# An mLSTM and top-2 expert kernel: the second half of the decay product moves to the states' bank and behind the logits, and five smaller edits

## The chip, the cores and the metric

The kernel runs on one core of a Trainium2 chip. The time is the device time of one execution in microseconds (us); before the change it was 513.11 us, the median of 3 runs (511.17 to 516.01). The core has five engines that take their instructions in order, each from its own queue: TensorE (PE, matrix products; its weight loads are shown as PEld), VectorE (DVE), ScalarE (ACT), GpSimd (POOL) and SyncE (SP, which only starts transfers here; POOL and ACT can start them too). An engine waits for another by semaphores.

## The reference

Two stages follow each other. The first is an mLSTM: for 4 batches and 8 heads a state of 40 x 40 runs through 768 steps, with an exponential input gate and a stabilised forget gate.

```python
for t in range(S):                        # B, H, S, D = 4, 8, 768, 40
    m_new = np.maximum(f_gate[:, :, t] + m, i_gate[:, :, t])
    f_stab = np.exp(f_gate[:, :, t] + m - m_new)
    i_stab = np.exp(i_gate[:, :, t] - m_new)
    C = f_stab * C + i_stab * outer(vt, kt)
    n = f_stab * n + i_stab * kt
    y[:, :, t] = sigmoid(o_gate) * (C @ qt) / max(abs(n . qt), 1)
```

Its 3072 rows of 320 values (8 heads x 40) go into a mixture of experts: `logits = x @ w_gate` plus a noise term that also needs `x @ w_noise`, the two best of 8 experts for each row, and for each expert `relu(x[mask] @ w1[e]) @ w2[e]`, weighted and added up. w1 is 320 x 1024 and w2 1024 x 320 for each expert.

## The kernel before, in words

**Units.** The mLSTM is computed in chunks of L = 64 steps. 768 steps are 12 chunks, and a unit `u` (24 of them) is one chunk of two batches; the two batches are the index `p` of all code below and lie in the two halves of the 128 partitions. Inside a chunk the recurrence is a masked matrix product, between chunks the 40 x 40 states are handed on. The parts of a unit are:

- `e_part(u, ps_)`, L305: the decay product. For each `p` one matmul of 98 rows by 512 columns (L312) of two operands LE and RE gives the exponents of the decays of 64 steps by 8 heads in a bank of the accumulator, and ACT takes the exponential into `w` (L315). Half 0 is `p` = 0, half 1 is `p` = 1. The accumulator's banks are named: `e` for the decay product, `st` for the states, `xt` for transposes and logits, `o` for outputs, `s` for scores (two of two banks). A bank asked for again must first have been read by everybody who uses it.
- `s_part`: the scores, 32 small matmuls and 8 larger ones on PE. `k_part` (L344) and `p_part` (L350, L354): DVE multiplies keys and scores by `w`, into `kd` and `p`.
- `c_part`, L356: 32 small matmuls build the new states in bank `st` (L364), and ACT copies the two batches' states into the next unit's `vk` (L367, two instructions).
- `o_part` (L373): 32 small matmuls give the outputs. `f_part` (L378 to L385): DVE divides, POOL multiplies by the output gate into `xr` (L385). `sig_part` (L320 to L322): three ACT instructions for the output gate.
- `keep_rows` (L388) writes `xr` to DRAM, `t_part` (L396) transposes it on PE, `tc_part` (L400) copies the transposes on ACT, `l_part` (L416) forms the logits on PE.

**Order.** Nothing is scheduled by a planner: each engine does its work in the order in which the Python code emits it. A turn `i` of the loop at the end of the listing works on several units at once: it ends the states and outputs of unit `i`, forms the decays and scores of unit `i + 2` (LEAD is 2), transposes `xr` of unit `i - 1` and forms the logits of unit `i - 2`. Routing (`fill`, `act`, `route`) is put between these parts in small steps: besides, at turn 6 ACT makes five constants, and at six even turns from 8 on it splits a piece of w1 (`split_w1`, L144; POOL makes the low half, L145).

**Gates.** The gates of all steps come by `fi` into `fit` (tile `raw`), in three loads; DVE works them out in pieces of 128 steps (`gate_math`, a scan, sums and a second scan, L193 to L212) into `HL`. Two chunks' worth of them at a time is moved into the operands by `gate_move(k)`, two transfers (L221 into `le`, L222 into `re`); there are two copies of the operands, so move 2 goes where move 0 was and waits until units 0 and 1 have formed their decay products. Moves 0, 1 and 2 serve units 0 and 1, 2 and 3, 4 and 5. The constant rows of RE are made once: `operands` (L228, ACT) and `heads(j, p, engine)` (L235 on ACT, L237 on DVE).

**Rows of the first expert.** Once the ranks of the first 12 units are known, `gather(0, 0, ...)` (L749, POOL) fetches the rows of expert 0 from DRAM by a list of row numbers, one transfer for each 128 rows, three in all, while the last units still run. After the units come the expert layers, a long run of large matmuls.

## Time and profile before

| | |
|---|---|
| median of the runs, us | 513.11 (511.17 to 516.01, n = 3) |
| the profiled execution's own time, us | 511.25 |
| span of its profile, us | 509.5 |
| PE busy | 494.4 us, 97% |
| DVE, ACT, POOL busy | 65%, 49%, 46% |
| PE's decay products | from 11.3 to 121.4 us |
| expert layers | from about 124 us on |

The span is the part of an execution that the profile covers, so 1.75 us of the execution's time lie outside it. PE is busy nearly all the time; the share of the other engines is that over the whole span, and in the units they are busier (the windows below). [...] A timeline row has its start, its length, the engine, the line and the operation, and in brackets the idle time of the engine just before it with the instruction that ended it. "SPq" is the queue of SP.

### The profile page before, as it was taken

To read this page: it belongs to the slowest core of one execution; us is meant where nothing else is said; L and a number is where in the kernel's file an instruction comes from. 1 tells how busy PE (TensorE), PEld (TensorE's weight loads), DVE (VectorE), ACT (ScalarE), POOL (GpSimd) and SP (SyncE) were. 2 spreads that over 40 slices of the span, in tenths; PEclk is the share of its full clock that TensorE was granted. 3 is DMA by queue.
4 is the path that set the end of the run, shared out by engine and by line. 5 is a ranking of instruction groups with operands and counts; after the bars stand their busy time and mean duration, and the time that the engine had idled before them with its cause. 6 is when DMAs were issued, how large, how long until landed. Compare 5 with 4: busy or idle time off the path is not lost.

```text
span 509.5 us, 13368 instructions
## 1 busy us (share of the span) xinstructions
PE 494.4 (97%) x5118; PEld 467.9 (92%) x5118; DVE 331.5 (65%) x891; ACT 248.3 (49%) x598; POOL 233.4 (46%) x313
## 2 busy tenths in 40 slices
PE   8899999999999999999999999999999999999993
PEld 3688888878999998999999999999999999999993
DVE  7998897975987779544853675376448347546310
ACT  6979989978533456414531543254145325415200
POOL 8545686874224863157134605531570453151033
PEclk9989999998999999999999999999999999999998
DMA  6899999988684583495058417723941782461033
GB/s 167 198 250 248 240 252 242 240 218 299 213 261 157 105 177 122 85 278 94 25 108 268 98 28 204 172 68 74 283 87 43 182 187 71 81 158 23 1 41 41
DMA packets 41274, 77.54 MB, mean 152 GB/s; under 512 B 10645, under 2 KB 31068, under 8 KB 39412
## 3 DMA queue, kind: packets, MB, share of 16 engines
q1 hardware_dynamic: 29316, 54.15, 37.5%
q0 software_dynamic: 11616, 20.57, 21.2%
q10 hardware_dynamic: 272, 1.90, 1.1%
q8 instruction: 42, 0.69, 0.6%
q14 instruction: 28, 0.23, 0.1%
HBM read 52.42 MB, written 17.40 MB: 137 GB/s over the span
## 4 chain that ended last, share of the span: by engine, by line
PE 76%; DMA 9%; POOL 4%; issue 3%; DVE 3%; ACT 3%; SPq 1%; POOLq 0%; DVEq 0%; ACTq 0%
PE s L997 25%; DMA y_out<-y,tok 7%; PE e L997 6%; PE o L1025 4%; PE o L1026 4%; PE o L1024 4%; PE o L373 4%; PE st L1025 4%; PE st L1026 4%; PE st L1024 4%; PE e L312 3%; PE s L336 3%; PE st L364 2%; POOL y_out L1052 2%; PE xt L416 2%
## 5 line engine op out<-in xcount | busy, mean ns | idle before, releaser
L1052 POOL DMA_INDIRECT y_out<-y,tok x53 | 87.3, 1647 | 183.1 <-DVE y L1042 180.5
L1009 ACT ACTIVATE hh<-s 128x384 fp32r<-128x384 f32 (+3 forms) x109 | 51.5, 472 | 114.1 <-PE s L997 113.1
L997 PE MATMUL s<-xh,w1h 128*128 128x384 f32 (+6 forms) x327 | 91.8, 336 | 0.0
L1012 DVE SCALAR_TENSOR_TENSOR hlo<-s,hh 128x384 fp32r<-128x384 f32 (+3 forms) x109 | 57.8, 530 | 35.6 <-ACT hh L1009 23.1
L997 PE MATMUL s<-xh,w1l 128*128 128x384 f32 (+6 forms) x327 | 74.1, 335 | 0.0
L749 POOL DMA_INDIRECT xg<-rows,tok x53 | 55.2, 1042 | 27.5 <-issue 14.7
L997 PEld LDWEIGHTS s<-xh,w1h 128*128 128x128 f32 x327 | 58.9, 188 | 1.3
L997 PEld LDWEIGHTS s<-xh,w1l 128*128 128x128 f32 x327 | 57.2, 188 | 1.5 <-DVE xh L783 0.2
L1025 PE MATMUL o<-w2l,hh 128*128 128x320 f32 x184 | 56.8, 309 | 0.0
L1026 PE MATMUL o<-w2h,hlo 128*128 128x320 f32 x184 | 56.8, 308 | 0.0
L1024 PE MATMUL o<-w2h,hh 128*128 128x320 f32 x184 | 56.1, 305 | 0.0
L997 PE MATMUL s<-xl,w1h 128*128 128x384 f32 (+6 forms) x218 | 55.4, 335 | 0.2 <-DVE xl L782 0.2
L1026 PE MATMUL st<-w2h,hlo 128*128 128x320 f32 x168 | 51.9, 309 | 0.0
L1025 PE MATMUL st<-w2l,hh 128*128 128x320 f32 x168 | 51.8, 308 | 0.0
L1024 PE MATMUL st<-w2h,hh 128*128 128x320 f32 x168 | 51.2, 305 | 0.0
L1042 DVE TENSOR_SCALAR y<-o,gw 128x320 f32<-128x320 f32 x22 | 12.1, 551 | 43.4 <-PE o L1026 43.4
L997 PEld LDWEIGHTS s<-xl,w1h 128*128 128x128 f32 x218 | 38.8, 188 | 1.3 <-DVE xl L782 0.4
L385 POOL TENSOR_TENSOR xr<-tm,vk 128x320 f32<-128x320 f32 x24 | 21.1, 880 | 31.6 <-DVE tm L384 7.0
L1042 DVE TENSOR_SCALAR y<-st,gw 128x320 f32<-128x320 f32 x20 | 11.0, 551 | 37.6 <-PE st L1026 37.6
L1024 PEld LDWEIGHTS o<-w2h,hh 128*128 128x128 f32 x184 | 34.5, 188 | 0.0
L1025 PEld LDWEIGHTS o<-w2l,hh 128*128 128x128 f32 x184 | 34.5, 187 | 0.0
L1026 PEld LDWEIGHTS o<-w2h,hlo 128*128 128x128 f32 x184 | 34.5, 187 | 0.0
(248 smaller groups left out, 1177.2 us busy)
## 6 DMA issues: line engine op xcount, KB each, us to landing
vk<-vk_in SPq DMA_DIRECT2D x48, 242.0 KB
raw<-w_in SPq DMA_DIRECT2D x6, 1536.0 KB
raw<-w_in SPq DMA_DIRECT2D x7, 1280.0 KB
qk<-qk_in SPq DMA_DIRECT2D x46, 128.0 KB
y_out<-zrow SPq DMA_DIRECT2D x15, 320.0 KB
rows<-xr POOLq DMA_DIRECT2D x23, 160.0 KB, 4.7
xt__2790<-xb SPq DMA_DIRECT2D x40, 72.0 KB
xt__2790<-xb SPq DMA_DIRECT2D x48, 48.0 KB
```

The source lines that it names most:

```text
L312: T.matmul(ps, LE[j][0:KE, c, 64 - 64 * p:192 - 64 * p], RE[j][0:KE, p, :, c * L:c * L + L], start=True, stop=True)
L373: T.matmul(OQ[u][half[p], h, :], PP[u][n, p, h, :], VK[u % 4][p][n, h * 41:h * 41 + 41], start=True, stop=True)
L385: P.tensor_mul(XR[u], tm.rearrange("p h d -> p (h d)"), SG[u % 4])
L749: P.indirect_dma_start(out=XG[0:rows_of(e, t), t], out_offset=None, in_=XD[0:n], in_offset=bass.IndirectOffsetOnAxis(ap=token(e, t), axis= ...
L997: T.matmul(ps[:, 0:n], l, r, start=i == 0, stop=i == len(ops) - 1)
L1009: A.activation(hi, x, AF.Relu)
L1012: V.scalar_tensor_tensor(lo, x, 0.0, hi.bitcast(F32), op0=OP.max, op1=OP.subtract)
L1024: T.matmul(ps, HH[:, j, c], W2H[:, j], start=j == 0, stop=False)
L1025: T.matmul(ps, HH[:, j, c], W2L[:, j], start=False, stop=False)
L1026: T.matmul(ps, HLO[:, j, c], W2H[:, j], start=False, stop=j == 7)
L1042: V.tensor_scalar(y[0:n], ps[0:n], GW[e][0:n, t:t + 1], None, op0=OP.mult)
L1052: st = P.indirect_dma_start(out=out, out_offset=bass.IndirectOffsetOnAxis(ap=token(e, t), axis=0), in_=y[0:n], in_offset=None, compute_op= ...
```

## The change

1. **Decay product.** From unit 3 on, half 1 of the decay product goes into bank `st`, which it shares with the states, not into `e`, which it shared with half 0. It stands directly behind the logits and the rank products of a turn and ahead of the transposes and the scores; its exponential on ACT stands directly behind that of half 0. In turn 0 (unit 2) it stays behind the scores and in `e`. `sig_part(i + 1)` is now last of the turn's decay and gate work on ACT.
2. **Gathers.** The three gathers are no longer emitted as two and one at the head of a turn, but singly: one at the head of a turn and one behind `f_part`.
3. **Gate rows.** The second load of gates (steps 128 to 383) is the third transfer of the kernel, where it was behind the first unit's keys and queries and a load of constants.
4. **Move 1 and keys of unit 2.** `gate_move(1)` is emitted ahead of `load_unit(2, "k")` on SP's queue.
5. **Move 2** is started by SP, where POOL did.
6. **Head sums.** `heads(1, 0)` is done by ACT, between the exponentials of units 0 and 1, where DVE did it; `heads(1, 1)` now comes behind those of unit 1.

```diff
     SP.dma_start(fit[:, :, 0:128], fi[:, :, 0:128])
     SP.dma_start(cet, ce)
+    SP.dma_start(fit[:, :, 128:384], fi[:, :, 128:384])
...
     load_unit(0, "k")
     SP.dma_start(cs[:, 0:128], cst[:, 0:128])
-    SP.dma_start(fit[:, :, 128:384], fi[:, :, 128:384])
     load_unit(0, "v")
...
-    load_unit(2, "k")
     operands(1, None, A)
     operands(1, 0, A)
     run(gate_math(GC * L, 256))
     gate_move(1)
-    heads(1, 0, V)
+    load_unit(2, "k")
...
         for p in ps_:
-            ps = XTB if first and p else psum.tile([128, 512], F32, name="e")
+            ps = XTB if first and p else psum.tile([128, 512], F32, name="st" if p and u > LEAD else "e")
...
     e_part(0, first=True)
     s_part(1)
+    heads(1, 0, A)
+    e_part(1, first=True)
     heads(1, 1, A)
-    e_part(1, first=True)
     operands(1, 1, A)
...
         if begun and late < len(tiles(0, 0)):
-            gather(0, 0, tiles(0, 0)[late:late + 2])
-            late += 2
-            begun = 2
+            gather(0, 0, tiles(0, 0)[late:late + 1])
+            late += 1
...
         f_part(i, lambda: fill(0.15, False))
+        if begun and late < len(tiles(0, 0)):
+            gather(0, 0, tiles(0, 0)[late:late + 1])
+            late += 1
         if i < 2:
             gate_steps(4)
         if i == 0:
-            gate_move(2, (P, P))
+            gate_move(2)
         t = l_part(i)
         w = r_part(t)
         b = None if w else b_part(t)
         if i:
+            e_part(i + LEAD, (1,))
             t_part(i - 1)
             tc_part(i - 1)
         lc_part(i, t, w)
         bc_part(t, b)
         s_part(i + 2)
         act()
-        if i:
-            sig_part(i + 1)
-        e_part(i + LEAD, (1,))
         if i == 0:
-            sig_part(1)
+            e_part(LEAD, (1,))
+        sig_part(i + 1)
```

On PE, turn 1 of the loop stood so before (states and outputs of unit 1, half 0 of unit 3, transposes of unit 0, scores of unit 3, half 1 of unit 3, states of unit 2):

```order
L364 MATMUL st<-vk_105,kd 40x41 x16
L373 MATMUL o<-vk_105,p 64x41 x16
L312 MATMUL e<-re_93,le_95 128x512
L396 MATMUL xt<-cs,xr 128x128 x3
L333 MATMUL s<-qk_103,cs 64x256 x2
L336 MATMUL s<-qk_103 64x64 x8
L333 MATMUL s<-qk_103,cs 64x256 x2
L336 MATMUL s<-qk_103 64x64 x8
L312 MATMUL e<-re_93,le_95 128x512
L364 MATMUL st<-vk_106,kd 40x41 x16
```

and now so:

```order
L363 MATMUL st<-vk_105,kd 40x41 x16
L372 MATMUL o<-vk_105,p 64x41 x16
L311 MATMUL e<-re_93,le_95 128x512
L311 MATMUL st<-re_93,le_95 128x512
L395 MATMUL xt<-cs,xr 128x128 x3
L332 MATMUL s<-qk_103,cs 64x256 x2
L335 MATMUL s<-qk_103 64x64 x8
L332 MATMUL s<-qk_103,cs 64x256 x2
L335 MATMUL s<-qk_103 64x64 x8
L363 MATMUL st<-vk_106,kd 40x41 x16
```

The second of the two decay products has moved from behind the scores to directly behind the first, and writes bank `st`; later turns have six logit matmuls (L416) between the two. Lines of the changed program are one lower here.

On ACT the first units stood so before (the exponentials of unit 0, head sums, those of unit 1, an operand, the state copies of unit 0, and half 0 of unit 2):

```order
L315 ACTIVATE w<-e 128x512
L315 ACTIVATE w<-xt 128x512
L235 ACTIVATE re_93<-raw_115 32x1024
L315 ACTIVATE w<-e 128x512
L315 ACTIVATE w<-xt 128x512
L228 ACTIVATE re_93<-raw_115 64x1024
L367 ACTIVATE vk_105<-st 40x328 x2
L315 ACTIVATE w<-e 128x512
```

and now so:

```order
L314 ACTIVATE w<-e 128x512
L314 ACTIVATE w<-xt 128x512
L235 ACTIVATE re_93<-raw_115 32x1024
L314 ACTIVATE w<-e 128x512
L314 ACTIVATE w<-xt 128x512
L235 ACTIVATE re_93<-raw_115 32x1024
L228 ACTIVATE re_93<-raw_115 64x1024
L366 ACTIVATE vk_105<-st 40x328 x2
L314 ACTIVATE w<-e 128x512
```

One instruction L235 more stands ahead of the state copies.

On POOL the gathers stood so before, at turns 19 and 20 (rows to DRAM, gathers, output of unit 19; then again for unit 20):

```order
L388 DMA rows<-xr 128x320
L749 DMA xg<-rows,tok 128x336 x2
L385 TENSOR_TENSOR xr<-tm,vk_107 128x320
L388 DMA rows<-xr 128x320
L749 DMA xg<-rows,tok 128x336
L385 TENSOR_TENSOR xr<-tm,vk_104 128x320
```

and now so:

```order
L387 DMA rows<-xr 128x320
L749 DMA xg<-rows,tok 128x336
L384 TENSOR_TENSOR xr<-tm,vk_107 128x320
L749 DMA xg<-rows,tok 128x336
L387 DMA rows<-xr 128x320
L749 DMA xg<-rows,tok 128x336
L384 TENSOR_TENSOR xr<-tm,vk_104 128x320
```

The second gather has moved from ahead of the output of unit 19 to behind it.

## Rows read from the trace of the kernel before

**Rows 1.** Windows (start:end in us, length, busy time of each engine, clock, DMA):

```profile
core 0: us, PE busy (x) PEld busy (x) DVE busy (x) ACT busy (x) POOL busy (x), PEclk, DMA share, GB/s
13.00:15.00 2.00, 0.87 (x13) 0.37 (x7) 1.96 (x4) 1.98 (x3) 1.78 (x5) 1.00 0.58 125
26.45:32.53 6.08, 6.08 (x116) 5.26 (x116) 5.67 (x12) 3.93 (x9) 2.72 (x4) 0.72 0.96 238
40.00:100.00 60.00, 59.37 (x1473) 51.94 (x1472) 52.67 (x149) 53.01 (x135) 42.34 (x72) 1.00 0.97 241
111.71:118.89 7.18, 6.21 (x120) 5.13 (x116) 3.45 (x7) 4.08 (x10) 5.07 (x6) 0.76 0.76 206
124.00:500.00 376.00, 375.49 (x2433) 369.12 (x2432) 227.68 (x633) 145.74 (x360) 149.01 (x174) 1.00 0.51 127
```

**Rows 2.** Chain of waits, 20 to 48 us (start, length, what ran):

```profile
22.57 3.75 DMA re<-hl
...
37.11 0.43 PE e L312
37.54 0.58 PE xt L416 x6
38.12 0.37 PE xt L396 x3
...
41.69 0.43 PE e L312
```

**Rows 3.** Timeline of PE, first units and units 19 to 21:

```profile
14.94 0.81 PE L364 MATMUL st<-vk,kd 64*40 64x41 f32 x32 [1.13 <-DVE kd L344]
...
23.12 0.50 PE L312 MATMUL e<-re,le 98*128 98x512 f32 x1 [0.24 <-ACT w L315]
...
26.45 0.47 PE L312 MATMUL e<-re,le 98*128 98x512 f32 x1 [1.15 <-DMA re<-hl]
...
111.71 0.50 PE L312 MATMUL e<-re,le 98*128 98x512 f32 x1
...
113.76 0.84 PE L396 MATMUL xt<-cs,xr 128*128 128x128 f32 x3 [0.97 <-POOL xr L385]
...
118.89 0.51 PE L312 MATMUL e<-re,le 98*128 98x512 f32 x1
```

**Rows 4.** Timeline of ACT:

```profile
12.96 1.14 ACT L235 ACTIVATE re<-raw 32x1024 fp32r<-32x1024 f32 x1
...
16.32 0.90 ACT L367 ACTIVATE vk<-st 40x328 f32<-40x328 f32 x2
17.85 0.60 ACT L315 ACTIVATE w<-e 128x512 f32<-128x512 f32 x1 [0.64 <-PE e L312]
...
21.68 0.90 ACT L367 ACTIVATE vk<-st 40x328 f32<-40x328 f32 x2
...
40.96 0.89 ACT L367 ACTIVATE vk<-st 40x328 f32<-40x328 f32 x2
...
59.82 0.89 ACT L367 ACTIVATE vk<-st 40x328 f32<-40x328 f32 x2
```

**Rows 5.** Timeline of DVE, gates and first unit:

```profile
7.95 0.48 DVE L193 TENSOR_TENSOR_SCAN xg<-raw,xg 64x128 f32<-64x128 f32 x1 [1.03 <-DMA raw<-fi_in]
...
11.26 0.90 DVE L237 TENSOR_SCALAR re<-raw 32x1024 fp32r<-32x1024 f32 x1
...
14.09 0.79 DVE L344 TENSOR_TENSOR kd<-vk,w 128x640 f32<-128x640 f32 x1
```

**Rows 6.** Timeline of POOL at the gathers:

```profile
111.47 1.31 POOL L749 DMA_INDIRECT xg<-rows,tok  x1 [0.30 <-issue]
112.85 0.86 POOL L385 TENSOR_TENSOR xr<-tm,vk 128x320 f32<-128x320 f32 x1
```

**Rows 7.** Timeline of SP's queue, first units:

```profile
19.54 0.60 SPq L157 DMA_DIRECT2D vk<-vk_in  x1
20.23 2.44 SPq L153 DMA_DIRECT2D qk<-qk_in  x4
```

## The prediction

> **What bounds the kernel now.** I read the windows first. In the expert layers PE is busy 375.49 of 376 us, at full clock and without gaps, and nothing there is changed [rows 1]. The whole of it starts when the last units end, so what the units win or lose is passed on to the end of the program, one for one. In the units, from 40 to 100 us, PE is busy 59.37 of 60 us [rows 1]: the chain of waits runs over PE alone, with 4.58 us from one decay product to the next (37.11 to 41.69) [rows 2]. So the other engines' times don't count there, except where one of them is late. That leaves the places where PE waits. The timeline of PE has three large ones: 1.13 us for `kd` before 14.94, 1.15 us for move 2 before 26.45, and 0.97 us for `xr` before 113.76 [rows 3]. The reader is to see a second cost behind two of them: the granted clock is 0.72 from 26.45 to 32.53 and 0.76 from 111.71 to 118.89, but 1.00 around the wait of 1.13 [rows 1]. [...] The turn from 26.45 to 32.53, from one half 0 to the next, took 6.08 us [rows 1] where an ordinary one takes 4.58 [rows 2]: 1.5 us more, with no wait inside.

> **The change, part by part.** The sum is made against the profiled execution's own time of 511.25, which is 1.86 under the median of 513.11; I carry the difference over to the median.

> *Gathers.* Before, POOL did two gathers ahead of `xr` of unit 19; the second ran from 111.47 to 112.78 and `xr` from 112.85 [rows 6], and PE waited 0.97 for that [rows 3]. The turn from 111.71 to 118.89 took 7.18 us against 4.58 normally, 2.60 lost, of which 0.97 is the wait and the rest the lower clock [rows 1, 3]. Now one gather stands ahead. `xr` can start when the first gather has been issued, 0.30 before the second began at 111.47, thus at about 111.2 (`tm` was long done), and ends at 112.1. PE asks for it behind the logits and the half decay product, which now stands ahead of the transposes: at 113.76 - 0.97 + 0.43 = 113.2. Margin 1.1. What is late next: the second gather now stands behind `xr` and with the rows to DRAM (an issue, 0.6 as in [rows 7]) and the third gather (1.31 by the row of the second) ahead of `xr` of unit 20. From 112.1: 0.3 + 1.3, 0.3 + 0.6, 0.3 + 1.3, then 0.86 of `xr`: it ends at about 117.1 at worst, and PE asks at 113.2 + 4.6 = 117.8. Margin 0.7. Gain **-2.6**; bounds 0 (the stall only moves) and -2.6.

> *First units.* DVE is rid of L237 (0.90) and gets the gate rows earlier, where it waited 1.03 [rows 5]: the load is issued third and no longer eighth. Together 1.9, but `kd` of unit 0 can't start before unit 0's exponentials end, at 12.96 [rows 4]; so it starts 1.1 earlier than 14.09 [rows 5]. PE is free at 14.94 - 1.13 = 13.81 [rows 3], so that wait goes, and outputs of unit 0 and half 0 of unit 2 come 1.1 earlier. That is not kept. ACT has 1.14 more to do (a second L235) ahead of the state copies of unit 0, which began at 16.32 with no idle time before them [rows 4]; now 17.46 to 18.36. The exponential of unit 2 began at 17.85 after 0.64 of idle time [rows 4]; now 18.4, 0.55 later. All of ACT's queue behind it shifts so: the copies of unit 1, 21.68 to 22.58 [rows 4], end at 23.1. Half 1 of unit 3 now needs bank `st`, so it waits for these copies: half 0 of unit 3 ends near 21.5, and PE has a **hole of 1.6 us** until 23.15. From there the old rows give the rest: from the transposes at 38.12 to 41.69 there are 3.57 us [rows 2], with one half product in it as now. Half 0 of unit 4 comes at 26.7, where it came at 26.45: **+0.3**. The hole is longer than the two waits that were followed by the lower clock, so I take that as before (0 change).

> *Move 2 by SP.* It stood on POOL, issued at 22.57 for `re` and landing 3.75 later [rows 2]; PE waited for it. SP is free at 20.14, ahead of unit 4's four loads [rows 7]. Two issues at 0.7 put `re` at about 20.9; landing 3.75 later is 24.7, not late for 26.7, and half as long again would still do. Those loads start at 21.6, not 20.23, and their 2.44 us of issues end at 24.0; the scores of unit 4 need them at about 28.5, so 4.5 us cover them. Cost 0; at worst, if SP's queue makes the move as late as POOL's was, the old wait stays. Move 1 ahead of the loads of unit 2: 4 issues, hidden by the same gap.

> *Half 1 in bank `st`, from unit 4 on.* The instructions are the same, in another order, and PE has 0.63 us idle in 60 [rows 1], so a gain is bounded by 1.0 us over all units. A loss: half 1 must wait until ACT has copied the states. It stands 0.43 + 0.58 = 1.01 behind half 0 [rows 2]; in an ordinary turn the copies end at 40.96 + 0.89 = 41.85 [rows 4], 0.16 behind half 0 at 41.69: margin 0.85. With a piece of w1 between, they ended at 60.71 [rows 4], and half 0 of that turn stands at 41.69 + 4 x 4.59 = 60.05, so half 1 comes at 61.06: margin 0.35. Only at turn 6, with five constants on ACT, do I expect a wait, of **+0.3**. For the shared bank the nearest row is the wait of 0.24 at 23.12 [rows 3], where half 1 waited for ACT; times 21 units that bounds the loss at 5. I take 0 for the others, since the margins are positive.

> [...] The two halves shared one bank until now, with a wait of up to 0.24 and a clock of 1.00 [rows 1, 3]. [...]

> Sum: +0.3 + 0.3 - 2.6 = -2.0: 509.25 for the profiled execution, **511.1** for the median.

> **The rivals.**
> - *A, the forecast*: 511.1, chance 0.42.
> - *B, the hole at unit 3 opens, but the clock stays at its upper level.* For it: the wait of 1.13 at 14.94 cost no clock. Against: both later waits did. -2.0 - 1.5 = -3.5: 509.6, chance 0.20.
> - *C, the hole does not open*, since ACT's copies come earlier than I place them or the head sums lie in idle time of ACT. Then the wait of 1.15, its 1.5 and the 2.6 all go: -5.2, 507.9, chance 0.12.
> - *D, the gather's stall moves to unit 20*: against it a margin of 0.7 only. The 2.6 are lost elsewhere and +0.6 is left: 513.7, chance 0.10.
> - *E, slower: the shared bank makes PE wait for late copies*, in the turns where ACT has more to do: the constants, six pieces of w1, two of routing, nine turns. Each wait of 0.2 and the lower clock behind it (1.5) make 15.3, and with the rest +13: 526. It decides if the copies end more than 1.0 behind half 0. For it: ACT is busy 53.01 of 60 us [rows 1], so extra work is seen at once. Against: the 0.35 left with a piece of w1, and that 0.24 of waiting drew no lower clock by itself. Chance 0.07.
> - The remaining 0.09 is the runs' own spread (511.17 to 516.01), with no mechanism.

> **How the numbers follow.** The likeliest is A, 511.1. C less 1.4 of spread gives the low end, 506.5; D plus 1.8 the high end, 515.5; E lies outside. A measurement of this kernel can tell about 1% from no change: below 508.0 or above 518.2. Faster by that is C for the most part (0.10), with the low ends of B (0.03) and of the rest (0.03): 0.16. Slower is E: 0.07. Within 1%: 0.77.

> **What would show it.** In the profile after: (1) no wait for `xr` from 110 to 120 us and turns of 4.6 there (else D); (2) a wait of 1 to 2 us of the half 1 product of unit 3 on ACT's state copies, near 21.5 to 23.2, and none for move 2 (else C); (3) a low clock behind it (else B); (4) DVE's `kd` of unit 0 near 13.0; (5) from 40 to 100 us PE's busy time stays at 59 of 60 and its clock at 1.00 (else E). I am wrong if the decay product's new place changes the period of 4.58, for which I have no row: every turn counts it 20 times.

## The result and the profile after

The changed kernel is **slower by 0.5%**: 515.61 us in the median of 20 runs against 512.36 us for 20 runs of the kernel before, ratio 1.0052 with a 95% interval of 1.0026 to 1.0077. The ratio leaves out the slow runs, those over 1.5% above the fastest of their kernel (three of the changed kernel's 20), so it is not the quotient of the medians. I had forecast 511.1 for a median of 513.11, which is a ratio of 0.996. The profiled execution took 513.57 us, and before 511.25. Each ratio below is to runs of the kernel before in the same sitting (a set of runs taken together on one chip).

The windows of the changed kernel, to be read beside those of [rows 1], are the first view. "PEclk" is the clock that TensorE was granted, as a fraction of the full one. In these two profiles it stands at 1.00 or at 0.50, and a stretch at 0.50 in the units lasts 3.41 us (49.62 to 53.03 here, 28.54 to 31.95 and 113.87 to 117.28 before).

```profile
core 0: us, PE busy (x) PEld busy (x) DVE busy (x) ACT busy (x) POOL busy (x), PEclk, DMA share, GB/s
40.00:100.00 60.00, 56.38 (x1394) 50.81 (x1392) 50.42 (x145) 49.88 (x128) 39.27 (x68) 0.97 0.99 239
48.58:54.46 5.88, 5.88 (x116) 5.18 (x116) 3.77 (x6) 3.98 (x10) 3.80 (x8) 0.71 0.98 232
82.94:87.38 4.44, 4.44 (x118) 4.04 (x116) 2.78 (x6) 3.48 (x10) 4.01 (x7) 1.00 0.96 263
124.00:500.00 376.00, 375.03 (x2498) 369.39 (x2493) 228.27 (x632) 147.27 (x365) 147.13 (x172) 1.00 0.51 130
```

From 40 to 100 us PE is busy 56.38 of 60 us, where it was 59.37: it waits 3 us more. The turn from 48.58 to 54.46 has no wait in it, but a clock of 0.71 and 5.88 us. An ordinary turn, though, now takes 4.44 us (82.94 to 87.38), not 4.58. The last column but one was there to be read before too, and I did not read it: the transfers are busy 0.97 (before) and 0.99 (changed) of the time from 40 to 100 us, and 0.51 in the expert layers.

Where PE waited in the units is in its timeline (rows with a wait alone):

```profile
12.36 0.47 PE L311 MATMUL e<-re,le 98*128 98x512 f32 x1 [0.66 <-DMA re<-hl]
...
19.93 0.51 PE L311 MATMUL e<-re,le 98*128 98x512 f32 x1 [0.87 <-ACT w L314]
...
24.06 0.50 PE L311 MATMUL st<-re,le 98*128 98x512 f32 x1 [1.52 <-ACT vk L366]
...
42.44 0.55 PE L372 MATMUL o<-vk,p 104*64 104x41 f32 x11 [0.96 <-issue]
...
48.58 0.47 PE L311 MATMUL e<-re,le 98*128 98x512 f32 x1 [1.16 <-issue]
...
76.15 1.13 PE L372 MATMUL o<-vk,p 64*64 64x41 f32 x32 [0.75 <-DVE tm L383]
...
81.88 1.13 PE L372 MATMUL o<-vk,p 104*64 104x41 f32 x31 [0.73 <-issue]
...
117.89 0.27 PE L335 MATMUL s<-qk 64*64 64x64 f32 x2 [0.26 <-issue]
...
123.69 0.68 PE L335 MATMUL s<-qk 64*64 64x64 f32 x16 [0.53 <-issue]
```

The waits for move 2 and for `xr` [rows 3] are gone, and the hole of 1.5 us that I expected for half 1 of unit 3 is there, before 24.06. The new ones say "issue": nothing that the profile shows released them. The first lies in the middle of 32 small matmuls that have all their inputs. What fits them is PE's own program. The section on queues has instructions as transfers:

```profile
q1 hardware_dynamic: 29430, 54.19, 37.3%
q0 software_dynamic: 11536, 20.53, 21.2%
q10 hardware_dynamic: 272, 1.90, 1.1%
q8 instruction: 42, 0.69, 0.6%
```

Queue q8 brings 42 packets, 0.69 MB: 16 KB each. I took their start and end from the packet records of the two traces, and counted PE's matmuls, weight loads and semaphore instructions up to each "issue" wait. The waits stand at the 1473rd, 1729th, 3265th, 5057th, 5313th and 5569th instruction: all multiples of 256 apart. If a packet of 16 KB is one such step of 256 instructions (my estimate from the distances), 42 packets hold 10752, and the trace has 10415 of PE's. The row does not say for which engine they are; by these counts I take them for PE's blocks of instructions, and the waits for waits at the ends of blocks. Around three such ends (us):

```
kernel, place   PE passes end before   packet starts   has landed   PE passes this end
before, 1473          36.35                37.28          38.53       41.23, no wait
changed, 1473         36.32                39.89          40.97       42.44, waited 0.96
changed, 1729         42.44                45.70          46.98       48.5,  waited 1.16
before, 3265          72.76                75.61          76.71       78.33, waited 0.48
changed, 3265         76.23                79.15          80.22       81.88, waited 0.73
```

(The sixth place, 5569, is passed at 129.8 us, behind the last row above.) In each of these waits PE goes on 1.4 to 1.7 us after the packet has landed, and in both kernels it passes no such end in the units sooner than 1.25 us after a landing. The packet takes 0.9 to 2.0 us itself; in these two profiles what differs is how late it starts. In the mean over 21 ends it starts 1.46 us after the end before in the kernel before, and 2.30 us in the changed one. The kernel before had one such wait too, 0.48 us before 78.33.

The first units stand on ACT and DVE as these two timelines show, beside [rows 4] and [rows 5]:

```profile
16.25 1.14 ACT L235 ACTIVATE re<-raw 32x1024 fp32r<-32x1024 f32 x1
...
18.49 0.90 ACT L366 ACTIVATE vk<-st 40x328 f32<-40x328 f32 x2
19.29 0.58 ACT L314 ACTIVATE w<-e 128x512 f32<-128x512 f32 x1
...
23.11 0.90 ACT L366 ACTIVATE vk<-st 40x328 f32<-40x328 f32 x2
```

```profile
6.85 0.47 DVE L193 TENSOR_TENSOR_SCAN xg<-raw,xg 64x128 f32<-64x128 f32 x1
...
14.04 0.82 DVE L343 TENSOR_TENSOR kd<-vk,w 128x640 f32<-128x640 f32 x1 [2.09 <-ACT w L314]
```

DVE's gates no longer wait (6.85, not 7.95), but `kd` is no sooner: it waits 2.09 us for ACT's exponentials, whose decay product came at 12.36. The state copies of unit 1 end at 24.0, and PE goes on at 24.06.

The gathers went as forecast; the timeline of POOL shows `xr` done before the second gather now, as against [rows 6], and PE did not wait for it:

```profile
113.19 1.70 POOL L749 DMA_INDIRECT xg<-rows,tok  x1 [0.31 <-DVE tm L383]
114.95 0.87 POOL L384 TENSOR_TENSOR xr<-tm,vk 128x320 f32<-128x320 f32 x1
115.98 1.06 POOL L749 DMA_INDIRECT xg<-rows,tok  x1 [0.15 <-issue]
```

### The profile page after: what moved, and what is told of

Same layout as the page of the kernel before. It is cut to its first block, busy times and chain, and to the rows that moved or that the text cites. A ratio compares the mean times of both kernels' runs of the same rounds, so it can differ in the third digit from the quotient of the medians.

```text
span 511.8 us, 13393 instructions
## 1 busy us (share of the span) xinstructions
PE 492.7 (96%) x5118; PEld 469.3 (92%) x5118; DVE 329.9 (64%) x890; ACT 249.6 (49%) x599; POOL 231.4 (45%) x311
## 4 chain that ended last, share of the span: by engine, by line
PE 80%; DMA 9%; ACT 3%; DVE 3%; POOL 2%; issue 2%; POOLq 0%; SPq 0%; DVEq 0%; ACTq 0%
PE s L998 26%; DMA y_out<-y,tok 7%; PE e L998 6%; PE o L1026 5%; PE o L1027 5%; PE o L1025 4%; PE st L1027 4%; PE st L1026 4%; PE st L1025 4%; PE o L372 4%; PE s L335 3%; PE st L363 2%; PE xt L415 2%; PE e L311 1%; PE xt L395 1%
## 5 line engine op out<-in xcount | busy, mean ns | idle before, releaser
L384 POOL TENSOR_TENSOR xr<-tm,vk 128x320 f32<-128x320 f32 x24 | 21.6, 898 | 32.8 <-DMA qk<-qk_in 9.9
```

The lines of the kernel that those rows point to most:

```text
L384: P.tensor_mul(XR[u], tm.rearrange("p h d -> p (h d)"), SG[u % 4])
```

## The experiments

Theory 1: the quicker turn meets transfers that are busy all the time, so PE's blocks of instructions come late (a "late block" is a wait of PE at the end of one), and the waits cost clock too. Theory 2: the edits of the first units put SP's transfers back, and that makes the blocks late. The table has the ratio to the kernel before, the mean granted clock over the compared runs (the kernel before had 0.990 in each of the four later sittings, 0.9898 to 0.9907), and the sum of PE's "issue" waits from 24 to 132 us in the one profile of each. Not all of these waits stand at the end of a block: 0.2 us of x2's, 0.5 of x1's, 0.8 of x3's, 0.4 of y1's, 1.1 of y3's and 0.4 of z1's don't, all between 114 and 122 us, and what ended those isn't known.

"Light" kernels leave out 320 KB of loads in each turn.

| kernel | ratio (95%) | clock | "issue" waits, us |
|---|---|---|---|
| before | 1 | 0.990 | 0.5 |
| changed, first sitting | 1.0052 (1.0026 to 1.0077) | 0.988 | 4.4 |
| changed, again (z3) | 1.0027 (0.9991 to 1.0063) | 0.987 | 3.1 |
| decay edit alone (x1) | 1.0014 (0.9982 to 1.0046) | 0.988 | 2.8 |
| gathers alone (x2) | 0.9962 (0.9927 to 0.9996) | 0.991 | 0.9 |
| first units alone (x3) | 0.9970 (0.9937 to 1.0004) | 0.994 | 1.7 |
| changed without decay edit (x4) | 0.9955 (0.9923 to 0.9987) | 0.995 | 1.0 |
| the same, again (z4) | 0.9991 (0.9967 to 1.0015) | 0.994 | 2.6 |
| the same, gate rows late too (y1) | 0.9973 (0.9948 to 0.9998) | 0.994 | 3.0 |
| changed, gate rows late (y2) | 1.0035 (1.0002 to 1.0067) | 0.987 | 4.7 |
| before, 64 KB a turn more (y3) | 1.0085 (1.0044 to 1.0126) | 0.983 | 1.7 |
| changed, light (z1) | 0.9921 (0.9887 to 0.9956) | 0.991 | 2.1 |
| without decay edit, light (z2) | 0.9932 (0.9904 to 0.9960) | 0.995 | 0.8 |
| changed, no hole (w1) | 1.0049 (1.0017 to 1.0082) | 0.988 | 4.5 |
| changed, no hole, light (w2) | 0.9923 (0.9895 to 0.9951) | 0.994 | 0.5 |

**x1_decay.** The decay edit (part 1) applied to the kernel before; its diff is the one shown above for `e_part` and its two calls.

> The kernel before with the decay product's edit alone (half 1 in bank st, behind the logits). Theory 1 (the quicker turn meets transfers that are already busy all the time, and PE's blocks of instructions come late): ordinary turns of 4.44 us, five or more waits of 0.4 to 1.3 us that end 1.3 to 1.7 us after a block of instructions has landed, 0.3 to 1.0% slower than before. Theory 2 (the first units' edits delay the transfers): turns of 4.44 us without such waits, 2 us quicker than before (0.996).

Ordinary turns took 4.44 us. Two late blocks made waits of 1.4 and 0.9 us, fewer than I expected (a third "issue" wait, 0.5 us at 116.2, is far from the end of a block); the loss, 0.14%, can't be told from none. Half 1 of unit 3 waited for the state copies here too, 1.19 us before 22.86. A chain of this kernel shows where the 0.14 us of a turn come from, beside that of the kernel before (0.37 for the transposes [rows 2], and for half 1, between the scores and the state products, the line here):

```profile
39.58 0.43 PE e L312
```

and with the decay edit:

```profile
82.57 0.43 PE e L312
83.00 0.58 PE xt L416 x6
83.58 0.33 PE st L312
83.90 0.33 PE xt L396 x3
...
87.01 0.43 PE e L312
```

Half 1 takes 0.33 here where it took 0.43, and the transposes behind it 0.33: each matmul is the same, only its neighbours are others.

The edit holds three things: the other bank, the place behind the logits, and `sig_part(i + 1)` behind the exponentials on ACT. No run takes them apart.

**x2_gather.** Part 2 alone.

> The kernel before with the single gathers alone. Both theories: no wait for xr at 113 us and no low clock there; 2 to 2.6 us quicker (0.995). At most one late block of instructions, as in the kernel before.

0.9962, and no wait for `xr`, as expected. Two late blocks, of 0.5 and 0.2 us, are one more than I expected.

**x3_start.** Parts 3 to 6 alone.

> The kernel before with the edits of the first units alone (gate rows third, move 1 ahead, move 2 by SP, head sums by ACT). Theory 1: the first decay product 1.0 us later, but no wait for move 2 and no low clock at 28 us; turns of 4.58 us; within 0.3% of before, no more late blocks of instructions than before. Theory 2: late blocks of instructions at turns 5 and 6, 2 to 4 us slower.

0.9970, and the highest clock up to here, 0.994; two late blocks, of 0.3 and 0.5 us. These edits alone cost nothing, so theory 2 falls as the reason of the loss.

**x4_nodecay.** The changed kernel with part 1 undone.

```diff
-            ps = XTB if first and p else psum.tile([128, 512], F32, name="st" if p and u > LEAD else "e")
+            ps = XTB if first and p else psum.tile([128, 512], F32, name="e")
...
-            e_part(i + LEAD, (1,))
             t_part(i - 1)
...
+        if i:
+            sig_part(i + 1)
+        e_part(i + LEAD, (1,))
         if i == 0:
-            e_part(LEAD, (1,))
-        sig_part(i + 1)
+            sig_part(1)
```

> The changed kernel without the decay product's edit. Theory 1: the gain of the single gathers stays, 2 us quicker than before (0.996), with at most two late blocks. Theory 2: as slow as the changed kernel (1.005), with late blocks at turns 5 and 6.

0.9955 here and 0.9991 in the later sitting. It is x4's profile, and z4's of the later sitting, that speak against a simple form of theory 1: nine and eleven ends of blocks were passed within 1.75 us of the landing (one before, eleven in the changed kernel), and the packets started 1.98 and 2.24 us behind the end before, in the mean, without the quicker turn.

**y1_nofi, y2_full_nofi.** The second load of gates back behind `cs`, without and with the decay edit.

```diff
     SP.dma_start(cet, ce)
-    SP.dma_start(fit[:, :, 128:384], fi[:, :, 128:384])
...
     SP.dma_start(cs[:, 0:128], cst[:, 0:128])
+    SP.dma_start(fit[:, :, 128:384], fi[:, :, 128:384])
```

> The changed kernel without the decay product's edit and without the early gate rows (single gathers, move 1 ahead, move 2 by SP, head sums by ACT). If the early gate rows only put SP's later issues back: first decay product at 11.3 us again and not 12.4, and 0.5 to 1 us quicker than with them (0.994 of before, where it was 0.9955). If they carry the gain of the first units: slower than 0.9955.

> The changed kernel without the early gate rows. Theory 1 (late blocks of instructions, from quicker turns on busy transfers): turns of 4.44 us and late blocks stay, 0.2 to 0.5% slower than before, about 1% slower than the same kernel without the decay product's edit. Theory 2 (the late start of the transfers is what the decay product's edit can't bear): no late blocks, 0.99 to 0.995 of before.

The first decay product came at 11.62 in y1 and at 12.50 in x4, and half 0 of unit 2 at 16.55 and 17.43, so the early gate rows do put the start back by 0.9, but the times can't be told apart (0.9973, 0.9955). y2 is slower than before, and 0.6% slower than y1 where I expected 1% (2.8 us by the means, with a 95% interval of 1.9 either way): the decay edit costs with the late gate rows too.

**y3_junk.** The kernel before with more to transfer.

```diff
+    JUNK = dram.tile([128, 128], F32, name="junk")
...
             load_unit(i + 3)
+            SP.dma_start(JUNK, w1[0, :, 0, 0:128])
```

> The kernel before with 64 KB more to transfer in each turn from turn 1 on (a copy in DRAM that nothing reads), its engines' work unchanged. Theory 1: PE's blocks of instructions start later (1.5 us behind the boundary before it in the kernel before, now 2.5 or more), and four or more of them are late, where one was; 0.5 to 2% slower. If instructions don't compete with the data: still one late block, and waits, if any, for data that is loaded.

0.85% slower, clock 0.983, with no work of PE, DVE, ACT or POOL changed. The packets start 2.07 us behind the end before (1.46 without, 2.5 expected), and seven ends are passed within 1.75 us of the landing, where one was. But only two blocks were late, by 0.4 and 0.2 us, where I expected four or more; the largest wait is move 2's, whose transfer is later still:

```profile
29.00 0.52 PE L313 MATMUL e<-re,le 98*128 98x512 f32 x1 [2.61 <-DMA re<-hl]
...
51.32 0.62 PE L417 MATMUL xt<-wgt,xts 128*128 128x16 f32 x5 [0.43 <-issue]
```

So more transfers make the kernel slower, but hardly by late blocks in this profile. SP's queue also starts one transfer more in each turn, and this run doesn't tell that from the 64 KB.

**y4_noqk, z1_after_light, z2_nodecay_light.** 320 KB less in each turn.

```diff
-            load_unit(i + 3)
+            load_unit(i + 3, "kv" if i < 4 else "v")
```

> The changed kernel with the loads of queries and keys left out from unit 7 on (older ones are used in their place, so the attention's values are others): 320 KB less in each turn. Theory 1: from turn 5 on no late block of instructions, each starts within 1 us of the boundary before it, all ordinary turns 4.44 us. If the late blocks come from PE's order itself: they stay.

> The changed kernel with the loads of queries and keys left out from unit 7 on (the attention's values are others), timed. If the decay product's edit loses only by late blocks of instructions on busy transfers: 1.5 to 3 us quicker than the kernel with the same loads left out and without that edit, and a mean granted clock as high as that one's. If its order or the shared bank costs clock by itself: as slow or slower, with the lower clock.

> The changed kernel without the decay product's edit, and with the same loads left out (the attention's values are others): the other half of the comparison. Turns of 4.58 us, no late blocks from turn 5 on; 1.5 to 3 us slower than with the edit if the transfers are the cause, quicker than it otherwise.

y4 and z1 are the same kernel. In y4's profile the packets start 1.20 us behind the end before, no end of turns 5 to 17 is near the limit, and the transfers' share is 0.77 from 40 to 100 us, where PE is busy 58.85 us:

```profile
40.00:100.00 60.00, 58.85 (x1492) 53.17 (x1493) 54.13 (x154) 53.80 (x138) 42.32 (x73) 1.00 0.77 185
```

In z1's, the same kernel at a share of 0.74, the packets start 1.76 us behind, and two blocks were late, at turns 5 and 6, where loads that were not left out still run; z2 had one, at turn 5. The timed pair failed my expectation: 0.9921 with the decay edit and 0.9932 without are the same; by the means the edit costs 0.3 us, 0.8 either way. At equal clock, by the mean of span times granted clock, z1 is 2.0 us quicker (505.8 and 507.8), as the shorter turn says; the lower clock (0.9909 and 0.9953) takes that back. With full transfers the same pair (z3, z4) stands at 509.1 and 509.3, with 0.9871 and 0.9944.

**z3_after, z4_nodecay.** The two kernels again, on that chip.

> The changed kernel once more, beside the one without the decay product's edit on one chip: 1.005 of before, mean granted clock near 0.987.

> The changed kernel without the decay product's edit once more: 0.9955 of before, mean granted clock near 0.994, 1% quicker than the changed kernel; at equal clock (time times granted clock) the two within 2 us of each other.

The means are 517.6 and 514.0 us: the decay edit costs 3.6 us, 1.3 either way. By the ratios, each to the kernel before, it is 0.36%, some 1.9 us, and not the 1% that I expected; the clocks came as expected, and so did the times at equal clock. On the same chip, in the same sitting, the edit cost 0.3 us with light transfers: that full transfers are a condition of the loss is shown by these four runs. In this profile of the changed kernel (timeline of PE) both kinds of wait come with the lower clock: it fell at 24.4 us, right behind the first, and at 55.1, within the second:

```profile
24.15 0.61 PE L311 MATMUL st<-re,le 98*128 98x512 f32 x1 [1.52 <-ACT vk L366]
...
55.84 0.59 PE L395 MATMUL xt<-cs,xr 128*128 128x128 f32 x2 [1.62 <-issue]
```

**w1_nohole, w2_nohole_light.** Half 1 of unit 3 stays in `e` and in its old place; the rest of the decay edit begins with unit 4.

```diff
-            ps = XTB if first and p else psum.tile([128, 512], F32, name="st" if p and u > LEAD else "e")
+            ps = XTB if first and p else psum.tile([128, 512], F32, name="st" if p and u > LEAD + 1 else "e")
...
+        if i > 1:
+            e_part(i + LEAD, (1,))
         if i:
-            e_part(i + LEAD, (1,))
...
-        if i == 0:
-            e_part(LEAD, (1,))
+        if i < 2:
+            e_part(i + LEAD, (1,))
```

> The changed kernel with half 1 of unit 3 left in bank e and behind the scores, as it was; the new order begins with unit 4. If the hole in turn 1 draws half of the clock loss: no wait of 1.5 us for the state copies near 24 us, mean granted clock near 0.990 (0.987 with the hole, 0.994 without the edit), 2 to 3 us quicker than the changed kernel, at or just under the time before (0.998 to 1.000). If the new order itself draws it: 0.987 and no more than 1 us quicker.

> The same with the loads of queries and keys left out from unit 7 on (the attention's values are others). If the hole draws the loss: mean granted clock near 0.995 (0.991 with the hole), time 0.988 to 0.990 of before, 1.5 to 2.5 us quicker than the light kernel without the edit (0.9932). If the order itself draws it: clock 0.991, time as with the hole (0.9921).

With light transfers the clock came up to 0.9941, nearer to the 0.9953 without the decay edit than to the 0.9909 with the hole. But the two sittings differ: w2's kernel before had 0.9907 and z1's 0.9898, and with that taken off the hole drew about half of the 0.0044. The time did not show it, with 0.9923 against 0.9921 (two chips, each within 0.004). With full transfers nothing was won, and my expectation of 2 to 3 us failed: 1.0049, clock 0.988, with late blocks of 4.5 us in all and eleven ends passed within 1.75 us of the landing. So the hole is not needed for the loss; that the late blocks are what makes it there is argued from this one profile.

Over all profiles with full transfers, the five with the decay edit have 2.8 to 4.7 us of "issue" waits and the six without it, y3 aside, 0.5 to 3.0. The packets start 1.96 to 2.48 us behind in the first and 1.46 to 2.24 in the second. The first are higher in the mean (3.9 and 1.6 us; 2.18 and 1.87), but the two sets overlap.

No version that computes the same beats the kernel before by more than 0.5%; x2, x4 and y1 have intervals that end just under 1. The one without the decay edit beats the changed kernel by 3.6 us, and before by 0.1 to 0.45% in two sittings, of which one has 1 in its interval.

## Why the prediction was wrong

**The step that failed** is "Half 1 in bank `st`, from unit 4 on". Apart from 0.3 us at turn 6 I put it at 0, and wrote that a gain is bounded by 1.0 us and that a loss would come from waits for state copies. It costs 3.6 us (z3 and z4) or 2.8 (y2 and y1); the rest of the sum, 2.3 us won, came as 0.45% and 0.09% (x4, z4), 2.3 and 0.5 us. Both sides of the step failed. The turn became 0.14 us shorter, which I had named as a sign of being wrong; over some 14 ordinary turns that is 2 us. I had taken "PE is busy 59.37 of 60 us" for "no gain possible", but a reordering can shorten the busy time too, as the rows of x1 show (0.43 to 0.33, 0.37 to 0.33). And the loss did not come from the state copies: beyond the hole no wait for them was over 0.32 us in any profile, and those at turn 6 (0.2 to 0.3 us in z3, y4 and w2) I had priced. The runs show in their place a loss that is 3.6 us with full transfers and 0.3 with light ones, at a lower mean clock (0.987, not 0.994). The largest new waits in the profiles, up to 1.79 us (before 55.26 in w1), are "issue" waits that I put down to PE's blocks of instructions, whose packets are among the transfers (q8). That these are how full transfers make the loss is the best account that I have; it is not shown by itself, since x4 and z4 have late packets too. I had asked of each engine who waits for it and did not ask it of the transfers, although the share of 0.97 stood in the window that I quoted [rows 1].

**The size.** By the means of z3 and z4 the decay edit costs 3.6 us, and its clock is lower by 0.0073. The stretch at the lower clock at 24.4 us in z3 lasted 3.41 us; at 0.50, as in the two profiles above, that costs half of it, 1.7 us, which is 0.0033 of the mean clock; by that estimate 0.0073 are 2.2 such stretches, 3.7 us. At equal clock the two kernels are level, so the 2 us that the shorter turns give are spent again on waits. Their two profiles have 7.1 and 5.4 us of PE's waits from 13 to 132 us, one with the hole of 1.52; how much of the rest is late blocks ("issue" 3.1 and 2.6) one profile each can't tell. With light transfers the edit gave its 2.0 us at equal clock and lost them to a lower clock, of which w2 puts about half on the hole.

**Rival E** had the right consequence, a slower kernel with a lower clock, and the wrong wait: I gave it 0.07, for waits on copies, at +13. The copies came within the 1.0 us between half 0 and half 1 almost everywhere. The shared bank is not enough by itself: w2 uses the banks in the same way from unit 4 on and had 0.9941. No run has the new place with the old bank, so the bank isn't excluded as a part.

**Gathers**: right. I said -2.6; alone they measured 0.9962, some 2 us, with an interval of 0.2 to 3.8. **The hole at unit 3**: right in cause and size, 1.52 us where I said 1.6, and 0.9 later than I placed it. I said the lower clock follows (A); in the first profile and in z1's it did not (B), in z3's and y4's it did, at 24.4 and 25.9. Whether it follows differs between executions, so A and B were not two cases but two faces of one. **First units**: two errors that made little. `kd` of unit 0 was not 1.1 earlier but at 14.04, where it was 14.09 [rows 5], because the first decay product came 1.0 later (12.36; it was at 11.35): the early gate rows pushed SP's later issues back, and move 0 with them, by 1.07. I moved the load ahead of five others and priced only what waited for it, not what it was moved past. **Move 2** was not late, as said. C and D did not occur.

**The range**, 506.5 to 515.5, was built on the spread of three runs and on E lying outside it. The median of 515.61 lies only 0.1 us above it, but 2.0 us won were forecast, and the ratio of 1.0052 is 2.7 us lost. The chance of "slower" was for a loss of 1%; what came is a loss of 0.3 to 0.5%, which 20 runs tell from none and three would not.

## What to carry to other kernels

Before costing a reordering on an engine that is busy all the time, look at the share of the transfers in the same window: where it was 0.97 before, the quicker turn lost 3.6 us here, and 0.3 with lighter transfers (0.74 in z1). What came late was, by the account above, the engine's own program. An "issue" wait in the middle of work that has all its inputs is worth a count of instructions: if such waits lie multiples of one number apart (of 256 here), look at the instruction queue's packets. And a wait on PE is priced with the clock that it may draw, as a chance per execution (here 1.7 us for a stretch of 3.41 at 0.50), which only a mean over many runs shows.

## What the runs showed of the hardware

In the 16 profiles the granted clock fell twenty times between 13 and 134 us (in the first two from 1.00 to 0.50), each time within a wait of PE of 0.36 us or more or 0.1 to 2.1 us behind its end. Many such waits were not followed by a fall (the hole of 1.52 us in the changed kernel's first profile, with 1.00 from 24 to 28 us).

A half product (98 x 512) took 0.33 us of x1's chain between logits and transposes (83.58; 0.32 a turn before, but 0.49 a turn behind, at 88.01) and 0.43 of the chain before between the scores and the state products (39.58), with operands of the same shape. What in the neighbours makes the 0.10 was not tried.

What stays open: which of the waits draw the lower clock and which don't (the same hole of 1.52 us did in z3 and not in the first profile); which part of the decay edit costs, the bank, the place or the order on ACT; how much of its loss is late blocks, and how much of y3's is move 2, SP's queue or the data.
